# Retention and a snake-activated feed-forward on one core: the place of one transpose among the loads, and of one square beside the last weight load

## The chip, the cores and the metric

The kernel runs on 1 core of one Trainium2 chip. The metric is the device time of one execution in microseconds (us). The core has five engines that this text names: TensorE (PE in the profile; its weight loads are PEld), VectorE (DVE), ScalarE (ACT), GpSimd (POOL) and SyncE (SP), which here does nothing but issue DMAs. Each engine works through its own list of instructions in order, and an instruction waits until what it needs has been done elsewhere.

## The reference: what is computed

Eight batches of a decayed causal attention without softmax (8 heads, 576 positions, 64 wide), then a feed-forward over the 4608 rows that come out:

```python
scores = scale * np.matmul(q, k.transpose(0, 1, 3, 2))
Dmat = np.where(rel >= 0, gamma[:, None, None] ** rel[None, :, :], 0.0)
x = np.matmul(scores * Dmat[None], v)        # then (batch, seq, heads * dim)
h = x @ w_in                                 # 4608 x 512 by 512 x 2048
s = np.sin(alpha * h)
g = h + s * s / (alpha + 1e-09)
out = g @ w_out                              # 2048 x 512
```

## The kernel before, in words

The 576 positions of a batch are taken as two parts of 256 (p = 0 and 1) and a rest of 64. The decay is put into q and k while they are cast to 16 bits (`cast`, L158), so scores need only a triangular mask; what lies over 128 positions back goes through running sums of k times v (`outer`, `more`, `to_state`, `add_states`).

**Attention of a batch b.** `load(b, nm, p)` (L137) issues the DMA of one part of q, k or v into a "raw" buffer, 512 KB; for k and v of batches 4 and later it is four DMAs of 128 KB. `cast` makes the 16-bit copy. q and k are then needed turned: in batches 0 and 1 TensorE does it (`turn`, L221, with `take` copying out), from batch 2 on a transposing DMA from SyncE (`crossed`, L213, issued at L217), which writes the tiles kT and qT. `scores` (L362) reads kT and qT of one part, `masked` multiplies by the mask on VectorE, `values` and `add_states` sum up the output, and `keep` puts it into xT, 512 rows of the feed-forward's input.

**Feed-forward of a block n** (512 rows, the main parts of batch n). For each of 16 feature chunks fc: `project` (L541) multiplies xT by a chunk of w_in, four matmuls; `sine` (L554) on ScalarE; `square` (L562) on the engine that is its third argument (A_ ScalarE, V VectorE, G_ GpSimd); `product` (L571) on VectorE, which writes the chunk of gT and frees the PSUM bank that `project` took. `gemm2(n, u, tag)` (L587) multiplies four chunks of gT by four rows of chunks of w_out: u = 4c + part, where part 3 reads chunks 12 to 15. `finish` copies the result out and stores it.

**The weights.** w_in and w_out come in quarters by DMAs that GpSimd issues and that turn 32 into 16 bits on the way (`load_w_in` L107, `load_w_out` L111). Quarter g of w_out is its chunks 4g to 4g + 3, so `load_w_out(3)` brings what part 3 of each `gemm2` reads; the first of these is `gemm2(0, 15)` (L843), then `gemm2(0, 7)` (L847).

**What sets the order.** Up to the middle of block 2 the order is written out by hand under `tc.manual_schedule()` (from L656): the calls stand in the order in which each engine is to take them, and each engine keeps the order of its own calls. From block 3 on a loop (L1140) places them. SyncE's list holds all loads of q, k and v, all transposing DMAs, the stores of `finish` and a few tiny DMAs named `gate` that hold SyncE back until a weight quarter has come (`wait_for_w_in`, `wait_for_w_out`). GpSimd's list holds casts, running sums, some squares and the weight loads. Which raw buffer a load takes is fixed by a string of digits (`BUFFERS`, L18); a load waits until the cast of the buffer's last content is done.

**Around the change.** In block 0, L790 to L803: chunk 10, its square on GpSimd, `load_w_out(3)`, `wait_for_w_in(3)` on SyncE, then chunk 14 with its square on ScalarE, chunk 12, and the first scores of batch 1. On SyncE, behind `wait_for_w_in(3)` stand the loads of batch 1's v part 0 (L811), k part 1 (L824) and v part 1 (L832); the cast of that k (L825) feeds `turn(1, "k", 1)` (L835) on TensorE. Around L869 to L880 SyncE issues the four transposes of batch 2 (k part 1, q part 1, k part 0, q part 0) with the load of batch 4's q part 1 ahead of the last, then loads of batches 3 and 4. The turned q part 0 of batch 2 is first read by `at[2].scores(0, 0, "m0")` (L947), behind `project(1, 0)` on TensorE; the load of batch 4's q part 1 is first read by `cast(4, "q", 1, G_)` (L997).

Of the kernel before, what the change touches and what calls it, by code (L numbers as in the profile page):

```python
# [35 lines left out]
def kernel(  # L36
# [68 lines left out]
    V, A_, G_ = nc.vector, nc.scalar, nc.gpsimd  # L105
# [5 lines left out]
    def load_w_out(g):  # L111
        nc.gpsimd.dma_start(w_out16[:, 4 * g : 4 * g + 4, :], w_out_r[:, g])

    def halves(n):
        return slice(64 * n, 64 * n + 64)
# [10 lines left out]
    def place(tag, shape, dtype):  # L126

        name = tag + next(slot_of[tag])
        if name not in places:
            places[name] = work.tile(shape, dtype, tag=name, bufs=1, name=name)  # L130
        return places[name]
# [5 lines left out]
    def load(b, nm, p):  # L137
        if p < 2 and b >= HALVED and nm != "q":
            t_ = place("raw", [P, H, 2 * D], F32)
            for g in range(2):  # L140
                for r in range(2):
                    s0 = 256 * p + 128 * g + 64 * r
                    nc.sync.dma_start(
                        t_[halves(g), :, r * D : r * D + D], src[nm][b, :, s0 : s0 + 64, :].rearrange("h i d -> i h d")
                    )
        elif p < 2:
            t_ = place("raw", [P, H, 2 * D], F32)
            nc.sync.dma_start(  # L148
                t_, src[nm][b, :, 256 * p : 256 * p + 256, :].rearrange("h (i r) d -> i h (r d)", r=2)
            )  # L150
        else:
            if b % 2 == 0:
                raw[b, nm, 2] = work.tile([P, H, D], F32, tag="raws", bufs=3, name=nm + "s32")
            t_ = raw[b - b % 2, nm, 2]
            nc.sync.dma_start(t_[halves(b % 2)], src[nm][b, :, 512:576, :].rearrange("h i d -> i h d"))
        raw[b, nm, p] = t_
# [47 lines left out]
    def new_T(b, nm, p):  # L204
        if (b, nm, p) not in T:
            T[b, nm, p] = (
                place(nm + "T", [P, 8, P], F16)
                if p < 2
                else work.tile([P, 4, P], F16, tag=nm + "Ts", bufs=B // 2, name=nm + "Ts")
            )  # L210
        return T[b, nm, p]

    def crossed(b, p, nms="kq"):  # L213
        for nm in nms:
            x = half[b, nm, p]
            x = x.rearrange("p a r t d -> p (a r t d)") if p < 2 else x.rearrange("p a t d -> p (a t d)")
            nc.sync.dma_start_transpose(new_T(b, nm, p), x)  # L217
# [323 lines left out]
    def project(n, fc, tag, part=None):  # L541

        if n not in gT:
            gT[n] = work.tile([P, FC, 512], F16, tag="gT", bufs=2, name="gT")
        if (n, fc) not in hps_of:
            hps_of[n, fc] = [bank(tag), None]
        cols = PART[part]
        for a in range(KT):
            matmul(  # L549
                hps_of[n, fc][0][:, cols], w_in16[fc // 4][:, a, fc % 4 :: 4], xs[n][:, a, cols],  # L550
                start=(a == 0 and part != 1), stop=(a == KT - 1), skip_group_check=True,
            )

    def sine(n, fc):  # L554
        hps = hps_of[n, fc][0]
        s_t = place("s", [P, 512], F16)
        nc.scalar.activation(  # L557
            s_t, hps, mybir.ActivationFunctionType.Sin, bias=0.0, scale=alpha_t[:, fc : fc + 1],
        )
        hps_of[n, fc][1] = s_t  # L560

    def square(n, fc, eng):  # L562
        s_t = hps_of[n, fc][1]
        ss_t = place("ss", [P, 512], F16)
        if eng is nc.scalar:
            nc.scalar.activation(ss_t, s_t, mybir.ActivationFunctionType.Square)  # L566
        else:
            eng.tensor_tensor(ss_t, s_t, s_t, MULT)  # L568
        hps_of[n, fc][1] = ss_t
# [41 lines left out]
    def wait_for_w_in(g):  # L611

        nc.sync.dma_start(gate, w_in16[g][:, 0, 0:64])
# [42 lines left out]
    with tc.manual_schedule():  # L656
# [133 lines left out]
        project(0, 10, "m0")  # L790
        sine(0, 10)
        square(0, 10, G_)
        load_w_out(3)
        wait_for_w_in(3)
        product(0, 5)
        project(0, 14, "h2")
        sine(0, 14)
        square(0, 14, A_)
        project(0, 12, "h1")
        sine(0, 12)  # L800
        at[1].scores(0, 0, "m1")
# [70 lines left out]
        cast(2, "k", 0, V)  # L872
        crossed(2, 1, "q")
        crossed(2, 0, "k")
        load(4, "q", 1)
        crossed(2, 0, "q")
        load(3, "v", 0)
        load(3, "v", 1)
        load(4, "v", 0)
# [381 lines left out]
```

## Time and profile before

| | us |
|---|---|
| median of 3 runs | 307.51 (306.63 to 307.99) |
| the profiled execution: its own time | 309.48 |
| the profiled execution: span of the trace | 307.5 |
| TensorE busy in the span | 293.8 |
| ScalarE, VectorE, GpSimd busy | 193.8, 190.1, 136.4 |

The profile is of one execution. Its page gives busy times by engine, the span in 40 slices with the clock that TensorE was granted (PEclk) and what the DMA engines moved, the chain of work that ended last, and groups of instructions. Other views of the same trace list an engine's instructions in order of time, with the idle time ahead of each and what ended it in brackets, or sum them over stretches. L numbers are lines of the kernel. A DMA's time from issue to landing is told where some instruction waited for it.

### The profile page before, as it was taken

What the parts mean: (1) busy time and instruction counts of PE and PEld (TensorE: products, weight loads), DVE (VectorE), ACT (ScalarE), POOL (GpSimd) and SP (SyncE); (2) the same over time, 40 slices, a digit from 0 to 9 for tenths busy, and PEclk for the clock granted to TensorE, in tenths of its full rate; (3) what the DMA queues carried; (4) which work ended last, traced back from release to release, by engine and by line L of the source; (5) the groups of instructions that cost most, each with busy time, mean ns of one, the idle gap of its engine ahead of it and who ended that gap; (6) DMA issues with size and microseconds to landing.
All of it is one profiled execution on the core that took longest, in us unless ns stands there. A gap on an engine that the chain in (4) does not pass through costs nothing.

```text
span 307.5 us, 7881 instructions
## 1 busy us (share of the span) xinstructions
PE 293.8 (96%) x3208; PEld 156.1 (51%) x3208; DVE 190.1 (62%) x280; ACT 193.8 (63%) x322; POOL 136.4 (44%) x151
## 2 busy tenths in 40 slices
PE   5889979969999999999999999999999999999995
PEld 4566445534554645454545444544455454444443
DVE  2678858766538786657764676566656746655600
ACT  1669916957686887684678567756774456555411
POOL 4793579472498686669058708563030000000000
PEclk9999999989999999999999999999999999999999
DMA  7999999998898688999597879877361121111133
GB/s 223 348 221 212 265 285 308 189 260 237 193 223 143 141 166 179 271 143 189 127 255 164 195 158 269 165 119 179 83 132 38 38 44 39 36 34 34 42 92 74
DMA packets 120484, 50.05 MB, mean 163 GB/s; under 512 B 80384, under 2 KB 115456, under 8 KB 120448
## 3 DMA queue, kind: packets, MB, share of 16 engines
q1 hardware_dynamic: 116928, 45.17, 62.6%
q0 software_dynamic: 2688, 4.19, 7.5%
q8 instruction: 25, 0.41, 0.6%
q10 hardware_dynamic: 832, 0.18, 0.3%
q14 instruction: 11, 0.09, 0.1%
HBM read 36.75 MB, written 9.44 MB: 150 GB/s over the span
## 4 chain that ended last, share of the span: by engine, by line
PE 82%; DMA 10%; POOL 3%; SPq 2%; issue 1%; ACT 0%; DVE 0%; DVEq 0%; ACTq 0%; POOLq 0%
PE ops L592 39%; PE hps L549 36%; DMA w_in<-in_moe_w_in_dram 4%; PE o L414 2%; DMA qT<-q 2%; SPq L148 2%; PE sc L372 2%; DMA raw<-in_q_dram 2%; DMA raw<-in_v_dram 2%; POOL q L194 1%; PE kv L308 1%; PE o L436 1%; POOL k L194 1%; POOL v L121 0%; PE os L497 0%
## 5 line engine op out<-in xcount | busy, mean ns | idle before, releaser
L573 DVE SCALAR_TENSOR_TENSOR gT<-ss,inva,hps 128x512 f16<-128x512 f16 x144 | 106.0, 745 | 64.0 <-ACT ss L566 58.9
L592 PE MATMUL ops<-w_out,gT 128*128 128x512 f16 (+2 forms) x592 | 142.5, 374 | 0.1
L557 ACT ACTIVATE s<-hps,alpha_t 128x512 f16<-128x512 f32 x144 | 97.6, 685 | 70.4 <-PE hps L549 68.3
L549 PE MATMUL hps<-xT,w_in 128*128 128x512 f16 (+1 forms) x532 | 127.5, 375 | 0.7 <-DMA w_in<-in_moe_w_in_dram 0.7
L549 PEld LDWEIGHTS <-w_in 128*128 128x128 f16 x596 | 66.9, 114 | 59.8 <-issue 2.0
L592 PEld LDWEIGHTS <-gT 128*128 128x128 f16 x592 | 56.0, 98 | 62.3 <-issue 0.4
L566 ACT ACTIVATE ss<-s 128x512 f16<-128x512 f16 x73 | 45.9, 631 | 1.4
L568 DVE TENSOR_TENSOR ss<-s 128x512 f16<-128x512 f16 x63 | 33.2, 528 | 20.4 <-ACT s L557 19.8
L194 POOL TENSOR_TENSOR k<-raw,cn 128x1024 f16<-128x1024 f32 (+1 forms) x17 | 30.5, 1795 | 27.1 <-DMA raw<-in_k_dram 27.1
L119 ACT COPY osb<-ops 128x512 f32<-128x512 f32 (+1 forms) x34 | 19.7, 580 | 16.6 <-PE ops L592 15.1
L194 POOL TENSOR_TENSOR q<-raw,cn 128x1024 f16<-128x1024 f32 x13 | 24.5, 1902 | 2.1 <-DMA raw<-in_q_dram 2.0
L384 DVE TENSOR_TENSOR ret<-sc,mask 128x1024 f16<-128x1024 f32 x16 | 19.1, 1218 | 3.7 <-PE sc L372 3.6
L353 POOL TENSOR_TENSOR s<-kvs,cn 128x256 f32<-128x256 f32 x21 | 13.3, 633 | 10.6 <-ACT kvs L119 10.4
L354 POOL TENSOR_TENSOR kvs<-s,kvs 128x256 f32<-128x256 f32 x21 | 15.3, 727 | 4.2 <-ACT kvs L119 1.7
L549 PE MATMUL hps<-xS,w_in 128*128 128x512 f16 x64 | 16.4, 379 | 0.0
L121 POOL CAST v<-raw 128x1024 f16<-128x1024 f32 x10 | 10.3, 1036 | 11.5 <-DMA raw<-in_v_dram 10.6
L384 DVE TENSOR_TENSOR ret<-sc,mask_halved 128x768 f16<-128x768 f32 x16 | 15.2, 949 | 0.0
L178 POOL TENSOR_TENSOR ks<-ks,cn 128x512 f16<-128x512 f32 x4 | 4.2, 1042 | 22.7 <-DMA vs<-in_v_dram 11.4
L119 ACT CAST xT<-o 128x1024 f16<-128x1024 f32 (+1 forms) x15 | 12.9, 878 | 1.7 <-PE o L436 1.6
L372 PE MATMUL sc<-qT,kT 64*64 64x128 f16 (+1 forms) x512 | 10.7, 219 | 2.5 <-DMA qT<-q 2.4
L346 POOL TENSOR_TENSOR s<-kvs,cn 128x256 f16<-128x256 f32 x17 | 10.9, 645 | 4.6 <-ACT kvs L119 3.0
L372 PEld LDWEIGHTS <-kT 64*64 64x64 f16 x512 | 7.8, 111 | 9.7 <-issue 8.4
(58 smaller groups left out, 148.3 us busy)
## 6 DMA issues: line engine op xcount, KB each, us to landing
out_dram<-osb SPq DMA_DIRECT2D x70, 128.0 KB, 2.5
raw<-in_q_dram SPq DMA_DIRECT2D x16, 512.0 KB, 5.9
raw<-in_k_dram SPq DMA_DIRECT2D x8, 512.0 KB, 6.1
raw<-in_v_dram SPq DMA_DIRECT2D x8, 512.0 KB, 6.2
raw<-in_v_dram SPq DMA_DIRECT2D x32, 128.0 KB, 3.2
raw<-in_k_dram SPq DMA_DIRECT2D x32, 128.0 KB, 3.3
w_in<-in_moe_w_in_dram POOLq DMA_DIRECT2D x4, 512.0 KB, 11.7
w_out<-in_moe_w_out_dram POOLq DMA_DIRECT2D x4, 512.0 KB, 13.0
```

The source lines that it names most:

```text
L119: eng.copy(d_, s_)
L194: eng.tensor_tensor(dst[:, a0:a1].rearrange("p a r t d -> p t (a r) d"), t_.rearrange("p (t a) x -> p t a x", t=2)[:, :, a0:a1].rearrange( ...
L353: nc.gpsimd.tensor_tensor(s32, self.kvs[:, c - 1], g1.unsqueeze(2).to_broadcast([P, 4, D]), MULT)
L354: nc.gpsimd.tensor_tensor(self.kvs[:, c], s32, self.kvs[:, c], ADD)
L372: matmul(sc[halves(g), t, c : c + n], kT[halves(t), 2 * a + r, halves(g)], qT[halves(t), 2 * a : 2 * a + 2, 64 * g + i0 : 64 * g + 64], st ...
L384: nc.vector.tensor_tensor(ret.rearrange("p t (z x) -> p (t z) x", z=2)[:, :, 0:n], sc.rearrange("p t (z x) -> p (t z) x", z=2)[:, :, 0:n], ...
L549: matmul(hps_of[n, fc][0][:, cols], w_in16[fc // 4][:, a, fc % 4 :: 4], xs[n][:, a, cols], start=(a == 0 and part != 1), stop=(a == KT - 1 ...
L557: nc.scalar.activation(s_t, hps, mybir.ActivationFunctionType.Sin, bias=0.0, scale=alpha_t[:, fc : fc + 1],)
L566: nc.scalar.activation(ss_t, s_t, mybir.ActivationFunctionType.Square)
L568: eng.tensor_tensor(ss_t, s_t, s_t, MULT)
L573: nc.vector.scalar_tensor_tensor(gT[n][:, fc, :], ss_t, inva[:, fc : fc + 1], hps, MULT, ADD)
L592: matmul(ops[n, c, cols.start][:, cols], gT[n][:, fk, c * P : (c + 1) * P], w_out16[:, fk, cols], start=(fk == 0), stop=(fk == FC - 1), sk ...
```

## The change

Two moves. The square of chunk 14 of block 0 goes from ScalarE to GpSimd, and `load_w_out(3)`, on GpSimd's list, comes behind that square instead of ahead of it; `wait_for_w_in(3)` is on SyncE's list and stands where it stood there. And on SyncE's list the load of batch 4's q part 1 comes behind the transpose of batch 2's q part 0 instead of ahead of it. The raw buffers and the s and ss buffers are taken in the same order as before.

```diff
@@ -790,12 +790,12 @@
         project(0, 10, "m0")
         sine(0, 10)
         square(0, 10, G_)
-        load_w_out(3)
         wait_for_w_in(3)
         product(0, 5)
         project(0, 14, "h2")
         sine(0, 14)
-        square(0, 14, A_)
+        square(0, 14, G_)
+        load_w_out(3)
         project(0, 12, "h1")
         sine(0, 12)
         at[1].scores(0, 0, "m1")
@@ -872,8 +872,8 @@
         cast(2, "k", 0, V)
         crossed(2, 1, "q")
         crossed(2, 0, "k")
+        crossed(2, 0, "q")
         load(4, "q", 1)
-        crossed(2, 0, "q")
         load(3, "v", 0)
         load(3, "v", 1)
         load(4, "v", 0)
```

## The prediction, made before the changed kernel was run

> **What bounds the kernel now.** First the page: the busy times and the span in 40 slices.
>
> ```profile
> PE 293.8 (96%) x3208; PEld 156.1 (51%) x3208; DVE 190.1 (62%) x280; ACT 193.8 (63%) x322; POOL 136.4 (44%) x151
> ...
> PE   5889979969999999999999999999999999999995
> ...
> PEclk9999999989999999999999999999999999999999
> ```
>
> TensorE is the bound: busy 293.8 us or 96% of the span, with the other engines under two thirds. It has holes only in the first quarter, and one slice there has a clock of 8 tenths. A change of a wait pays only where TensorE stands idle, so next I read TensorE in order of time there (start, duration, instruction, idle ahead of it and its releaser).
>
> ```profile
> 42.78 0.62 PE L227 MATMUL tr<-ident,k 128*128 128x128 f16 x8 [1.65 <-POOL k L194]
> ...
> 44.76 1.04 PE L592 MATMUL ops<-w_out,gT 128*128 128x512 f16 x4
> ...
> 66.99 0.64 PE L372 MATMUL sc<-qT,kT 64*64 64x128 f16 x16 [2.37 <-DMA qT<-q]
> ```
>
> Two holes: 1.65 us ahead of the turning of batch 1's k part 1, and 2.37 us ahead of `scores(0, 0)` of batch 2, which waits for the transposed q. The change touches both. The second, from 64.62 (66.99 - 2.37), costs more than its length. The stretches with the granted clock (the number behind POOL's) show it:
>
> ```profile
> 40.00:50.00 10.00, 8.25 (x184) 4.38 (x182) 6.67 (x9) 3.73 (x9) 8.21 (x8) 1.00 1.07 315
> ...
> 67.00:71.00 4.00, 4.00 (x26) 1.77 (x27) 1.88 (x2) 1.44 (x3) 3.69 (x7) 0.58 0.88 216
> ```
>
> Right behind the hole the clock is 0.58 of full over 4 us. Twelve projection matmuls take 4.08 us on the chain of work, where four take 0.86 elsewhere on it:
>
> ```profile
> 31.86 5.84 DMA raw<-in_v_dram
> ...
> 59.79 7.06 DMA qT<-q
> 67.63 4.08 PE hps L549 x12
> ...
> 95.21 0.86 PE hps L549 x4
> ```
>
> 3 x 0.86 = 2.58, so the slow clock costs 1.50 us. Hole and clock together: 2.37 + 1.50 = **3.87 us**. The hole of 1.65 us left the clock at full (the stretch from 40 to 50).
>
> **The second move: the transpose ahead of the load.** SyncE's list around it:
>
> ```profile
> 57.80 1.26 SPq L217 DMA_TRANSPOSE kT<-k  x1
> 59.16 0.54 SPq L148 DMA_DIRECT2D raw<-in_q_dram  x1
> 59.79 1.99 SPq L217 DMA_TRANSPOSE qT<-q  x1
> 61.88 2.26 SPq L148 DMA_DIRECT2D raw<-in_v_dram  x2
> ```
>
> SyncE issues without a gap here, so its pace, and no wait, sets these times. GpSimd has cast that q by 52.2 (50.27 + 1.90):
>
> ```profile
> 50.27 1.90 POOL L194 TENSOR_TENSOR q<-raw,cn 128x1024 f16<-128x1024 f32 x1
> ...
> 82.63 3.76 POOL L194 TENSOR_TENSOR q<-raw,cn 128x1024 f16<-128x1024 f32 x2
> ```
>
> The transpose is issued at 59.16 instead of 59.79: 0.63 us won by issue alone. More lies behind: ahead of it in the same queue are no longer 512 KB. What the queue moved from 58 to 62 us, in slices of 0.1 us:
>
> ```profile
> GB/s 289 257 294 292 289 289 108 161 289 289 289 274 262 282 279 276 292 289 353 266 259 88 39 49 67 77 54 108 123 97 97 102 56 61 143 113 179 230 102 108
> ```
>
> The transposes run at some 290 GB/s up to 60.1, then the load that stands between them begins at under 150. The last transpose has its data behind that load. It lands 7.06 us after its issue, while the page says what others take:
>
> ```profile
> kT<-k SPq DMA_TRANSPOSE x12, 5.0
> qT<-q SPq DMA_TRANSPOSE x12, 3.9
> ```
>
> Bounds for the moved one: 59.16 + 3.9 = 63.1, + 5.0 = 64.2, and + 7.06 = 66.2 if the load was not the reason. I take 3.9, since it now follows a transpose directly. TensorE is there at 64.62, so the hole is gone in the first two cases, and with it the slow clock: -3.87. In the third the hole shrinks by 0.63 to 1.7, which is the length of the hole that left the clock full: between -0.63 and -2.1. The load itself comes some 2 us later; its cast starts at 82.63 (the second row above), so nothing waits for it. The loads behind it keep their issue times, since the same instructions stand ahead of them.
>
> [...]
>
> What TensorE needs next, 3.87 us earlier? VectorE and ScalarE get their work from TensorE here. The first loads it meets are batch 3's v, issued by 64.1 (61.88 + 2.26). The two loads of that size below take 5.84 and 8.3, which makes 70 to 72.4. Their casts on ScalarE stand at 76.46, now 72.6:
>
> ```profile
> 76.46 1.56 ACT L119 CAST v<-raw 128x512 f16<-128x512 f32 x2
> ```
>
> Then come batch 3's transposes:
>
> ```profile
> 78.22 2.71 SPq L143 DMA_DIRECT2D raw<-in_k_dram  x4
> 81.44 0.40 SPq L148 DMA_DIRECT2D raw<-in_q_dram  x1
> ...
> 85.23 0.54 SPq L148 DMA_DIRECT2D raw<-in_q_dram  x1
> 86.42 1.38 SPq L217 DMA_TRANSPOSE qT<-q  x1
> ...
> 93.38 1.34 SPq L217 DMA_TRANSPOSE qT<-q  x1
> ```
>
> ```profile
> 93.60 0.64 PE L372 MATMUL sc<-qT,kT 64*64 64x128 f16 x32
> ...
> 100.32 0.42 PE L372 MATMUL sc<-qT,kT 64*64 64x128 f16 x16
> ```
>
> The scores at 93.60 move to 89.73 and read the q issued at 86.42. That issue waits for a GpSimd cast, which comes earlier with TensorE, but SyncE is itself nearly full from 60 on. What it can win are its gaps ahead of 81.44 (0.51 behind 78.22 + 2.71) and 86.42 (0.65 behind 85.23 + 0.54), of which some 0.1 each is no wait. So it issues at 85.5: + 3.9 gives 89.4, in time by 0.3; with 5.0 it would be late by 0.8. The scores at 100.32 move to 96.45; their q, issued at 93.38 by the same list, now at 92.4, lands at 96.3 to 97.4: late by 0 to 0.95. I take **+0.3** for this; its ends are 0 and, if SyncE gains nothing at all (93.38 + 3.9 to 5.0 against 96.45), 0.8 to 1.9. Later transposes hang on stores, which follow TensorE.
>
> **The first move: square and w_out's last quarter.** GpSimd's list:
>
> ```profile
> 33.39 1.04 POOL L568 TENSOR_TENSOR ss<-s 128x512 f16<-128x512 f16 x1 [0.57 <-ACT s L557]
> 34.37 0.60 POOL L112 DMA_DIRECT2D w_out<-in_moe_w_out_dram  x1
> 37.76 1.03 POOL L121 CAST v<-raw 128x1024 f16<-128x1024 f32 x1 [2.79 <-DMA raw<-in_v_dram]
> 38.76 0.60 POOL L346 TENSOR_TENSOR sS<-kvs,cn 128x256 f16<-128x256 f32 x1
> 40.82 1.90 POOL L194 TENSOR_TENSOR k<-raw,cn 128x1024 f16<-128x1024 f32 x1 [1.45 <-DMA raw<-in_k_dram]
> ```
>
> ```profile
> 33.92 0.63 ACT L566 ACTIVATE ss<-s 128x512 f16<-128x512 f16 x1
> ```
>
> ```profile
> 35.42 1.40 DVE L573 SCALAR_TENSOR_TENSOR gT<-ss,inva,hps 128x512 f16<-128x512 f16 x2
> ```
>
> The moved square takes 1.04 instead of 0.63, from 34.4, when GpSimd comes to it (its sine is done by 33.92, where ScalarE's square began), to 35.4. GpSimd has 2.79 us free ahead of 37.76, which hides it. ScalarE is rid of 0.63. The product waits to 35.45 where it began at 35.42: under 0.1, which VectorE makes up in its next idle time, and without that it would be 0.1 on the path. So these instructions cost nothing.
>
> What counts is that w_out's quarter is issued at 35.4, 1.05 us later. The loads of batch 1 move beside it. The k's time to landing; what was moved from 34 to 42 us, in slices of 0.2 us, with the last quarter's time; and the times of all four quarters of w_out:
>
> ```profile
> raw<-in_k_dram SPq DMA_DIRECT2D x1, 512.0 KB, 8.3
> ```
>
> ```profile
> GB/s 85 210 335 282 346 344 284 318 323 341 348 346 351 346 351 361 420 259 266 233 225 253 225 266 205 187 225 228 128 243 305 310 348 346 305 305 310 330 343 348
> ...
> w_out<-in_moe_w_out_dram POOLq DMA_DIRECT2D x1, 512.0 KB, 7.4
> ```
>
> ```profile
> DMA to landing us min/median/max: 7.4/13.0/15.8
> ```
>
> The v, 5.84 us in the chain above, lands at 37.70; the k 3.1 us behind it at 40.8, though issued (8.3 before) only 0.6 behind. The quarter moved meanwhile: from 37.4 to 39.8 the rate is down at 130 to 270. With it 1.05 later, the k's data may be through before. GpSimd can start on that k at 39.37 (38.76 + 0.60), so the gain at TensorE's first hole is between 0 and 1.45. For the other sign: the quarter is read at 44.76 and landed 7.4 us after its issue, which makes 42.8 now; 44.76 - 1.45 is 43.3, so it is in time. I take **-1.1**, nearer to the full 1.45, since 1.05 us at the 340 GB/s that were moved then is 0.36 MB, over half of that load.
>
> [...]
>
> **Sum.** -3.87 - 1.1 + 0.3 = -4.7. The execution's own time is 309.48 (span 307.5), so 304.8 there; against the median of the runs, 307.51, it is 302.8.
>
> **The rivals.**
> - The k is no earlier, because the quarter shares its engines anyway. For: its 8.3 us. Against: the quarter is 1.05 later. -3.87 + 0.3: 303.9.
> - Batch 3's transposes take the place of the wait: SyncE stays late and the scores at 96.45 wait for 98.3. For: SyncE's list has few gaps. Against: its three waits follow TensorE. -3.87 + 1.9 - (0 to 1.1): 304.4 to 305.5.
> - The swap does not do what it says: the transpose lands 7 us after issue for another reason. -0.63 if the clock still drops, -2.1 if not, and the first move's 0 to -1.1: 304.3 to 306.9.
> - The slow clock stays where it is though the hole is gone, because something other than the hole sets it. For: the hole of 1.65 left it full. Against: it begins with the matmul behind the hole. -2.37 - 1.1 + 0.3: 304.3.
> - Slower: w_out's last quarter comes too late for `gemm2(0, 15)` at 44.76. Place: TensorE's list at L843, with everything behind it. Price: the other quarters took 13.0 in the median and up to 15.8; 35.4 + 13.0 = 48.4 is a hole of 3.6, + 15.8 = 51.2 one of 6.4, each with the slow clock's 1.5 behind it: 3.6 + 1.5 - 3.87 + 0.3 = +1.5 and +4.3, 309.0 to 311.8. It decides from a landing near 48.4; one in 44.8 to 47 eats a part of the gain. Against: this quarter took 7.4, and it starts when no other quarter is left.
>
> **How the numbers follow.** Chances: forecast 0.41 (302.0 to 303.6), k no earlier 0.23, batch 3's transposes 0.13, slow clock stays 0.03, no effect of the swap 0.12, slower 0.08. Predicted 302.8. The range goes from 301.8 (-3.87 - 1.45 with no new wait is 302.2, and the runs spread by some 0.5 around their median) to 306.4, which leaves out a part of the third rival and the slower one. Faster by over 0.5% (1.5 us, about what a measurement can tell from no change) takes the first four cases and a third of the fifth: 0.84; same 0.08; slower 0.08.
>
> **What would show it.** Right: no idle time ahead of `scores(0, 0)` near 63 to 65 us, no slice of PEclk at 8; the transposed q lands under 5 us after its issue; GpSimd starts the k cast near 39.5 and the first hole is under 0.6 us. Wrong: a new idle time ahead of scores near 89 or 96, or ahead of L592 near 43.

## The result

The changed kernel takes 305.9 us in the median of 21 runs (303.88 to 311.41), against 307.59 for the kernel before, run beside it (21 runs, 305.43 to 309.5). That is 1.7 us less. The ratio is 0.9953, 95% interval 0.993 to 0.9976; it leaves out 1, but is just under the 0.5% that the forecast took as what a measurement can tell from no change. Executions over 1.5% above the fastest of their kernel are left out of all ratios, here two of the changed kernel's 21 (309.04 and 311.41); with them the means are 306.46 and 307.53, a ratio of 0.9965. Forecast were 4.7 us and 302.8.

The profiled execution after has an own time of 305.86 and a span of 303.9; before, 309.48 and 307.5. So this one pair shows -3.6 us, twice what the medians show. Most of what follows is about that difference.

The page of after, the lines that answer to those of before (busy times, TensorE's share in the 40 slices, its granted clock):

```profile
span 303.9 us, 7880 instructions
...
PE 292.6 (96%) x3208; PEld 156.2 (51%) x3208; DVE 189.2 (62%) x280; ACT 193.9 (64%) x321; POOL 136.5 (45%) x152
...
PE   6789989999999999999999999999999999999995
...
PEclk9999999999999999999999999999999999999999
```

ScalarE has one instruction less and GpSimd one more. The slice with a clock of 8 tenths is gone. TensorE in order of time (start, duration, instruction, idle ahead of it and its releaser):

```profile
41.52 0.62 PE L227 MATMUL tr<-ident,k 128*128 128x128 f16 x8
...
43.84 1.02 PE L592 MATMUL ops<-w_out,gT 128*128 128x512 f16 x4 [0.27 <-DMA w_out<-in_moe_w_out_dram]
...
46.22 0.45 PE L308 MATMUL kv<-v,k 64*64 64x64 f16 x32 [1.35 <-ACT v L119]
...
65.04 0.42 PE L372 MATMUL sc<-qT,kT 64*64 64x128 f16 x16
65.39 2.78 PE L549 MATMUL hps<-xT,w_in 128*128 128x512 f16 x12
```

Both holes of before are gone: there is no idle time ahead of the turning at 41.52 or of the scores at 65.04, and the twelve projection matmuls behind those scores take 2.78 where they took 4.08. Two new waits stand between: 0.27 us for w_out's last quarter and 1.35 us for the cast of a v. Together they are 1.62 us, as much as the first hole was (1.65). The chain of work of after names the v's load behind that cast:

```profile
33.50 11.60 DMA raw<-in_v_dram
45.12 1.05 ACT v L119
...
65.46 2.71 PE hps L549 x12
```

What the two moves did by themselves can be read on their engines. SyncE's list of after, then the DMA view of its window from 58 to 60 us (the number is the time from issue to landing):

```profile
57.61 1.26 SPq L217 DMA_TRANSPOSE kT<-k  x1
58.97 1.25 SPq L217 DMA_TRANSPOSE qT<-q  x1
60.27 0.58 SPq L148 DMA_DIRECT2D raw<-in_q_dram  x1
```

```profile
qT<-q SPq DMA_TRANSPOSE x1, 3.3
```

The transpose was issued at 58.97 and landed at 62.3, almost 3 us ahead of the scores; before it was 59.79 and 7.06. GpSimd's list of after, then the DMA view of its window from 31 to 38 us:

```profile
33.80 2.04 POOL L568 TENSOR_TENSOR ss<-s 128x512 f16<-128x512 f16 x2 [0.57 <-ACT s L557]
35.78 0.60 POOL L112 DMA_DIRECT2D w_out<-in_moe_w_out_dram  x1
...
39.57 1.89 POOL L194 TENSOR_TENSOR k<-raw,cn 128x1024 f16<-128x1024 f32 x1
```

```profile
raw<-in_k_dram SPq DMA_DIRECT2D x2, 512.0 KB, 6.7
w_out<-in_moe_w_out_dram POOLq DMA_DIRECT2D x1, 512.0 KB, 8.0
```

The quarter is issued at 35.78 instead of 34.37, the k lands 6.7 us after its issue instead of 8.3, and its cast begins at 39.57 without a wait. Each move did what it was meant to do in this trace.

### The profile page after: what moved, and what is told of

It reads as the page before. It is cut to its first block, busy times and chain, and to the rows that moved or that the text cites. A ratio compares the mean times of both kernels' runs of the same rounds, so it can differ in the third digit from the quotient of the medians.

```text
span 303.9 us, 7880 instructions
## 1 busy us (share of the span) xinstructions
PE 292.6 (96%) x3208; PEld 156.2 (51%) x3208; DVE 189.2 (62%) x280; ACT 193.9 (64%) x321; POOL 136.5 (45%) x152
## 3 DMA queue, kind: packets, MB, share of 16 engines
q0 software_dynamic: 2688, 4.19, 7.7%
## 4 chain that ended last, share of the span: by engine, by line
PE 85%; DMA 10%; ACT 1%; POOL 1%; SPq 1%; issue 1%; DVE 0%; DVEq 0%; ACTq 0%
PE ops L592 39%; PE hps L549 39%; DMA raw<-in_v_dram 4%; DMA w_in<-in_moe_w_in_dram 4%; PE o L414 2%; DMA raw<-in_k_dram 2%; PE sc L372 2%; PE kv L308 1%; SPq L148 1%; PE o L436 1%; POOL k L194 1%; ACT s L557 0%; ACT v L119 0%; POOL w_in L109 0%; PE os L497 0%
## 5 line engine op out<-in xcount | busy, mean ns | idle before, releaser
L194 POOL TENSOR_TENSOR k<-raw,cn 128x1024 f16<-128x1024 f32 (+1 forms) x17 | 28.8, 1696 | 26.2 <-DMA raw<-in_k_dram 25.6
L568 POOL TENSOR_TENSOR ss<-s 128x512 f16<-128x512 f16 x9 | 9.2, 1039 | 6.2 <-ACT s L557 6.2
L119 ACT CAST v<-raw 128x1024 f16<-128x1024 f32 (+1 forms) x6 | 5.8, 976 | 9.8 <-DMA raw<-in_v_dram 9.8
```

Of the source, the lines that this page charges most:

```text
L119: eng.copy(d_, s_)
L194: eng.tensor_tensor(dst[:, a0:a1].rearrange("p a r t d -> p t (a r) d"), t_.rearrange("p (t a) x -> p t a x", t=2)[:, :, a0:a1].rearrange( ...
```

## The experiments

**The theories.** A: the terms of the forecast were those of one execution that stood far above the median; typical executions stall less, so there is less to win. B: the moves win what was forecast, and batch 3's transposes, late by more than the forecast's 0.3, give most of it back. C: one of the two moves has no effect, or harms.

### Each move alone, and both kernels again

The edits are the two hunks of the diff, one at a time: r2 has only the second (transpose ahead of the load), r3 only the first (square and w_out's quarter); r1 is the kernel before, r4 the whole change.

> The kernel before, unchanged, looked at again with the granted clock of each execution. Theory A (the prediction's sum was made on an execution that is not typical: the slow clock behind the hole ahead of scores comes in some executions alone): the trace has the hole of 2 to 3 us near 65 us again, but most executions show a granted clock over 0.995 and the profiled time is 1 to 2 us under 309.5. Theory B (the slow clock is always there and the gain went elsewhere): a clock of about 0.994 in nearly every execution, twelve projection matmuls of 4.08 us behind the hole. Time the same as before in both, ratio 1.000 within 0.003.

> The second move alone: the transpose of batch 2's q part 0 ahead of the load of batch 4's q part 1; square and w_out's last quarter as before. Theory A: no idle time ahead of scores near 65 us, and 1.5 to 2.5 us faster than before, which is the hole without the slow clock; as fast as the whole change. Theory B: the slow clock goes too, -3.5 to -4 us in the runs. The prediction on record has -3.87 + 0.3 for this part. Theory C (the first move costs what the second wins): this one is 1 us or more faster than the whole change.

> The first move alone: the square of chunk 14 on GpSimd and w_out's last quarter issued behind it; SyncE's list as before. The prediction on record: -1.1 us. Theory A: the first hole only moves, from ahead of the turning of k (1.65 us) to ahead of the outer product (1.35) and of the product with w_out (0.27), because v part 1 lands 2 us later: 0 +- 0.4 us. Theory C: 1 us or more slower than before, the hole near 65 us being longer.

> The whole change again, on the same chip as its two parts. Theory A: the sum of the two parts, -1.5 to -2.5 us against before, with a trace that again has no idle time ahead of scores near 65 us and 1.3 to 1.9 us of it near 43 to 46. Theory B: -3.5 us. Theory C: 1 us or more slower than the second move alone.

| | median us | ratio to before | 95% interval |
|---|---|---|---|
| r1, before | 308.76 | 1.0034 | 1.0 to 1.0067 |
| r2, second move alone | 306.66 | 0.9967 | 0.993 to 1.0005 |
| r3, first move alone | 307.93 | 0.9993 | 0.9957 to 1.0029 |
| r4, both | 306.13 | 0.9965 | 0.993 to 1.0 |

Before's median beside these four is 307.38. r2 is 0.7 us under it and r4 1.2, where theory A had 1.5 to 2.5 for both and B 3.5 or more. The rows also show how far two runs of one kernel can lie apart: r1 is the kernel before, unchanged, and its median is 1.4 us above. So a difference of 0.3% in one run says little; that the whole change is faster rests on four runs of it that agree (0.9953, 0.9965, and 0.9968 and 0.9949 below).

r1's trace says more. TensorE, then the chain of work:

```profile
65.17 0.42 PE L372 MATMUL sc<-qT,kT 64*64 64x128 f16 x16 [1.85 <-DMA qT<-q]
...
90.90 0.64 PE L372 MATMUL sc<-qT,kT 64*64 64x128 f16 x32 [0.60 <-DVE ss L568]
```

```profile
58.12 6.91 DMA qT<-q
65.59 2.71 PE hps L549 x12
```

No hole near 42 us, a second hole of 1.85, and the twelve matmuls behind it at full clock (2.71). This execution took 306.86 us, 2.6 less than the one that the forecast was built on. In r3 the transpose is as late as before, and the stretch behind it (the granted clock stands behind the busy time of POOL) shows this:

```profile
66.11 0.42 PE L372 MATMUL sc<-qT,kT 64*64 64x128 f16 x16 [2.68 <-DMA qT<-q]
...
92.66 0.64 PE L372 MATMUL sc<-qT,kT 64*64 64x128 f16 x32 [1.45 <-DMA qT<-q]
```

```profile
67.00:71.00 4.00, 4.00 (x49) 2.03 (x48) 2.28 (x4) 3.35 (x6) 3.11 (x6) 1.00 0.76 158
```

A hole of 2.68, longer than the 2.37 of the forecast, and the clock stays full. For the second move, theory C is out by the traces: the second hole is there without it and gone with it. In r4, with both moves, only one wait is left, on batch 3's scores:

```profile
89.69 0.64 PE L372 MATMUL sc<-qT,kT 64*64 64x128 f16 x32 [1.35 <-DMA qT<-q]
```

### Before once more, the second move alone, and the whole change

> The second move alone, again, beside the whole change on one chip. In six traces the k load of batch 1 landed 6.7 us after issue in all that have the first move, and 6.7 or 8.3 to 9.4 in those that have not. Theory E (the first move takes away the k's late landing, which comes in a part of the executions only, and pays with v's): this one shows a first hole of 1.6 to 2.8 us in a part of its executions, and its mean time is 0.3 to 1.2 us over the whole change's, with more spread. If the first move is worth nothing: equal means within 0.3.

> The whole change once more, as the measure for the other three on this chip: 1.2 to 2 us under before, no idle time near 65 us, 0 to 1.4 us near 43 to 46 us and 0 to 1.4 us near 90 us.

> The kernel before, one look: which of its waits is in a typical execution. The prediction took 1.65 us ahead of batch 1's turning, 2.37 us ahead of batch 2's scores and 1.50 us of slow clock behind from one trace. Theory A: the wait of batch 2's scores is there again (1.5 to 2.8 us), the slow clock behind it and the first hole are not both. If the one trace was typical: both are there again.

> The kernel before, a further look, with the same question: the wait of batch 2's scores 1.5 to 2.8 us; the first hole either under 0.3 us, with batch 1's k landing 6.7 us after issue, or over 1.5 us, with 8.3 us or more.

> The whole change, as the measure for it on the same chip: 1 to 1.7 us under before.

The second move alone gave 0.9992 (0.9946 to 1.0038) this time, the whole change 0.9968 (0.9932 to 1.0004) in r12 and 0.9949 (0.9916 to 0.9982) in r16. The mean of r11 lies 1.0 us over that of r12 (307.48 against 306.48), as theory E expected. Its trace, of an execution of 305.36 us, has a first hole of 0.37 only, no second one, and this:

```profile
89.54 0.64 PE L372 MATMUL sc<-qT,kT 64*64 64x128 f16 x32 [1.14 <-DMA qT<-q]
```

r13 and r14 are one execution of before each, 309.34 and 310.3 us. The second hole of 1.5 to 2.8 us that was expected is smaller in both. r13, TensorE, then the stretches from 40 to 48 us, and its k's time to landing:

```profile
43.71 0.62 PE L227 MATMUL tr<-ident,k 128*128 128x128 f16 x8 [2.59 <-POOL k L194]
...
68.08 0.42 PE L372 MATMUL sc<-qT,kT 64*64 64x128 f16 x16 [0.90 <-DMA qT<-q]
```

```profile
40.00:44.00 4.00, 1.41 (x12) 0.59 (x9) 1.21 (x3) 0.72 (x1) 2.25 (x2) 1.00 1.10 322
44.00:48.00 4.00, 4.00 (x46) 1.78 (x43) 2.17 (x4) 0.33 (x1) 2.70 (x5) 0.57 1.04 307
```

```profile
raw<-in_k_dram SPq DMA_DIRECT2D x2, 512.0 KB, 9.2
```

Here the k is late by more, the slow clock stands behind the **first** hole, and the second hole is down to 0.90 because TensorE itself comes later. r14 has a third pattern:

```profile
42.14 0.62 PE L227 MATMUL tr<-ident,k 128*128 128x128 f16 x8 [1.02 <-POOL k L194]
...
65.20 0.42 PE L372 MATMUL sc<-qT,kT 64*64 64x128 f16 x16 [1.22 <-DMA qT<-q]
...
93.00 0.71 PE L372 MATMUL sc<-qT,kT 64*64 64x128 f16 x32 [2.66 <-DMA qT<-q]
```

In r16, the whole change, four small waits come together and the execution takes 306.92:

```profile
41.24 0.62 PE L227 MATMUL tr<-ident,k 128*128 128x128 f16 x8 [0.17 <-POOL k L194]
...
45.50 0.45 PE L308 MATMUL kv<-v,k 64*64 64x64 f16 x32 [1.24 <-ACT v L119]
...
64.69 0.42 PE L372 MATMUL sc<-qT,kT 64*64 64x128 f16 x16 [0.21 <-DMA qT<-q]
...
91.22 0.64 PE L372 MATMUL sc<-qT,kT 64*64 64x128 f16 x32 [1.39 <-DMA qT<-q]
```

These rows make a ledger. For each profiled execution it has TensorE's idle times in three places, an estimate of 1.50 us (the prediction's price) for each slow stretch of the clock behind a hole, and what its own time is without them.

| | own time | 40 to 48 us | 62 to 70 | 88 to 104 | slow clock | left |
|---|---|---|---|---|---|---|
| before, the forecast's | 309.48 | 1.65 | 2.37 | 0 | 1.50 | 303.96 |
| before, r1 | 306.86 | 0 | 1.85 | 0.60 | 0 | 304.41 |
| before, r13 | 309.34 | 2.59 | 0.90 | 0 | 1.50 | 304.35 |
| before, r14 | 310.30 | 1.02 | 1.22 | 2.66 | 1.50 | 303.90 |
| first move alone, r3 | 308.13 | 0.17 | 2.68 | 1.45 | 0 | 303.83 |
| second move alone, r11 | 305.36 | 0.37 | 0 | 1.14 | 0 | 303.85 |
| both, after | 305.86 | 1.62 | 0 | 0 | 0 | 304.24 |
| both, r4 | 305.26 | 0 | 0 | 1.35 | 0 | 303.91 |
| both, r12 | 305.46 | 0 | 0 | 1.24 | 0 | 304.22 |
| both, r16 | 306.92 | 1.41 | 0.21 | 1.39 | 0 | 303.91 |

The last column is the same within 0.6 us, while the own times differ by 5. So these executions differ by their stalls in these three places and by little else, and 304.1, the mean of that column, is about the time without them. The traces of r5 to r10 and r15 fit as well, from 303.72 (r15) to 304.41 (r10); r2's needs a fourth place, which is told further down. Against the medians, a typical execution of before stalls for about 307.59 - 304.1 = 3.5 us, one of after for 305.9 - 304.1 = 1.8. The forecast's execution stalled for 5.52.

### Batch 3's transposes ahead of a gate and a load

If theory B holds, taking away the wait near 90 us should bring back the missing microseconds. r5 adds this to the change (r6 does it without the first move):

```diff
-        wait_for_w_in(3)
-        load(4, "q", 0)
         crossed(3, 1, "q")
         crossed(3, 0, "k")
+        wait_for_w_in(3)
+        load(4, "q", 0)
         load(4, "k", 1)
```

> The whole change, and the same move once more for batch 3: on SyncE's list the transposes of its q part 1 and k part 0 come ahead of the tiny gate and of the load of batch 4's q part 0. Theory A (what the hole near 65 us gives is taken back by the wait of batch 3's scores near 90 us, since SyncE cannot follow): that wait, 1.35 us in the trace of the whole change on this chip, is gone or under 0.3, and the time is 0.7 to 1.5 us under the whole change's, 2 to 3 us under before. Theory B (the gain went elsewhere, to the slow clock alone): the time stays within 0.4 us of the whole change's 306.1.

> The second move and its repetition for batch 3, without the first move (square on ScalarE, w_out's last quarter issued ahead of it). If the first move is worth nothing, as the look at it alone says (ratio 0.999), this is as fast as the kernel with all three, within 0.4 us. The prediction on record has the first move at -1.1 us: then this is about 1 us slower than that one.

Both came out slower than before: r5 310.73 us, 1.0141 (1.01 to 1.0182); r6 310.28, 1.0102 (1.0054 to 1.015). The wait near 90 was gone. r5's GpSimd and TensorE show what stands in its place:

```profile
93.92 1.90 POOL L194 TENSOR_TENSOR q<-raw,cn 128x1024 f16<-128x1024 f32 x1 [4.19 <-DMA raw<-in_q_dram]
...
98.42 1.90 POOL L194 TENSOR_TENSOR k<-raw,cn 128x1024 f16<-128x1024 f32 x1
```

```profile
97.56 0.42 PE L372 MATMUL sc<-qT,kT 64*64 64x128 f16 x16 [0.92 <-DMA qT<-q]
...
100.37 0.44 PE L308 MATMUL kv<-v,k 64*64 64x64 f16 x32 [2.15 <-POOL k L194]
```

The load that now comes behind the transposes feeds `cast(4, "q", 0, G_)`; GpSimd waits 4.19 us for it, and the cast of a k that stands behind it in GpSimd's list makes TensorE wait 2.15, with a slow clock behind (0.50 from 101.5 to 104.7 us). With r5's 1.37 ahead of kv at 46.00 its ledger is 310.34 - 1.53 - 3.07 - 1.50 = 304.24 (1.53 with a 0.16 at 41.54). In r6, which lacks the first move, a first hole of 2.78 with its own slow clock (0.57 from 44 to 48 us) comes on top.

r10 (and r15, the same kernel) takes the cause away: to r5 it moves that one cast on GpSimd's list to behind `square(2, 13, G_)`. r9 keeps the load ahead and moves only the gate behind the transposes:

```diff
-        cast(4, "q", 0, G_)
...
         square(2, 13, G_)
+        cast(4, "q", 0, G_)
```

```diff
-        wait_for_w_in(3)
         load(4, "q", 0)
         crossed(3, 1, "q")
         crossed(3, 0, "k")
+        wait_for_w_in(3)
```

> The whole change with the tiny gate DMA (w_in's last quarter, long landed) behind batch 3's transposes of q part 1 and k part 0 instead of ahead of the load before them: SyncE comes 0.65 to 1.0 us earlier to that load and to the transposes, in the same order. Theory A (SyncE's list, not TensorE, sets when batch 3's q is there): the wait of the scores near 90 us is 0.6 to 1.0 us shorter than in the whole change, and the time 0.4 to 1.0 us under the whole change's. If that wait were set by something else, no change within 0.4 us.

> The kernel with batch 3's transposes ahead of the load of batch 4's q part 0, which came out 4 us slower than the whole change since GpSimd stood 4.2 us at the cast of that load with the cast of batch 4's k behind it. Here that cast comes behind the cast of k and a square on GpSimd. Theory A (GpSimd's order was the new wait): the 2.15 us ahead of the outer product near 100 us are gone, no slow clock there, and the time is 0.5 to 1.5 us under the whole change's. If the transposes' place itself was harmful: still 3 us or more over the whole change.

> The whole change with batch 3's transposes ahead of the load of batch 4's q part 0 and that load's cast behind the cast of batch 4's k: again, to tell it from the whole change, which it beat by 0.8 us in the mean with intervals that overlap. Theory A (part of the gain was taken back by batch 3's wait): 0.4 to 1.2 us under the whole change again. If that was chance: within 0.3 us of it.

r10 gave 306.29 us, 0.9933 (0.9891 to 0.9976), and its repeat r15 307.52, 0.9994 (0.9961 to 1.0027), which is 4.4 and 3.2 us under r5's median. So the cast was most of what r5 lost. But r16 beside r15 has 0.9949, so this kernel isn't shown to beat the change; its two runs lie 0.6% apart. r9 gave 306.49, 0.9986 (0.9947 to 1.0025), beside r12's 306.48. TensorE of r9 and of r10:

```profile
88.91 0.64 PE L372 MATMUL sc<-qT,kT 64*64 64x128 f16 x32 [0.51 <-DVE ss L568]
```

```profile
96.29 0.42 PE L372 MATMUL sc<-qT,kT 64*64 64x128 f16 x16 [0.97 <-DMA qT<-q]
```

The wait near 90 can be taken away, and then the next one shows: 0.51 for a square on VectorE, or 0.97 for the next q on SyncE's list. No time was gained that these intervals (some 0.8% wide) can show. Theory B, as the main cause, is out: there are not 3 us behind that wait. What the wait does cost, within the intervals, stays open.

### The second move the other way

r7 is the kernel before with a second load ahead of the transpose:

```diff
         load(4, "q", 1)
-        crossed(2, 0, "q")
         load(3, "v", 0)
+        crossed(2, 0, "q")
```

> The kernel before with two loads instead of one ahead of the transpose of batch 2's q part 0 (the load of batch 3's v part 0 too). Theory A (each load of 512 KB ahead of it in the queue is what makes it late): the hole near 65 us grows by 1 to 2 us, to 3 to 4.5 us, the transpose lands 1 us or more later, and the slow clock behind the hole comes in most executions since the hole is longer; 2 to 4 us slower than before, less what batch 3's scores no longer wait. Theory D (the transpose is late for another reason than the load): the hole grows by 0.6 us at most, what SyncE needs to issue the load.

It gave 309.95 us, 1.0065 (1.0009 to 1.012). TensorE, and the chain of work:

```profile
43.72 0.62 PE L227 MATMUL tr<-ident,k 128*128 128x128 f16 x8 [2.70 <-POOL k L194]
...
69.06 0.42 PE L372 MATMUL sc<-qT,kT 64*64 64x128 f16 x16 [1.39 <-DMA qT<-q]
```

```profile
61.41 7.51 DMA qT<-q
```

The transpose lands 7.51 us after its issue, against 6.35 to 7.06 in the five traces with one load ahead, so the second load adds little to the first; the 1 us or more of theory A isn't shown. The hole is only 1.39 because this execution had a first hole of 2.70 with a slow clock behind it (0.83 from 40 to 50 us), which made TensorE late as well. That first hole is not of r7's edit, so its ratio can't be put down to the load alone.

### The slower rival, made to happen

r8 is the change with w_out's last quarter issued later still:

```diff
         square(0, 14, G_)
-        load_w_out(3)
...
         cast(1, "v", 0, G_)
+        load_w_out(3)
```

> The whole change with w_out's last quarter issued later still, behind the cast of batch 1's v part 0 on GpSimd, near 39 us instead of 35.5. With the 6.3 to 8.0 us that this quarter took to land in the traces so far, it lands near 45.3 to 47 and the product that reads it first waits 1.5 to 3 us; batch 1's v part 1 lands 2 us earlier than in the whole change and nothing waits for it. 1 to 2.5 us slower than the whole change. If the quarter's place decides nothing (the rival that DMA engines share whatever is there), the time is within 0.5 us of the whole change.

It gave 309.2 us, 1.0071 (1.0031 to 1.0112): slower than before, and over 1% (some 3 us) slower than the whole change in its four runs, where 1 to 2.5 us were expected. TensorE:

```profile
46.80 1.86 PE L592 MATMUL ops<-w_out,gT 128*128 128x512 f16 x4 [2.54 <-DMA w_out<-in_moe_w_out_dram]
```

Four matmuls take 1.86 behind the hole, where they take 1.02 in after: the slow clock stands here too. The trace also has 0.77 us ahead of the turning of k and 0.83 ahead of batch 3's scores. The place of the slower rival (a hole at L843, and the slow clock behind it) was right. Its bound was not: the quarter landed at 46.8 (issued at 39.06, 7.70 to landing), where the forecast had a landing at 44.8 to 47 eat only a part of the gain. The change itself stops short of it, with a wait of 0.27.

## Why the prediction was wrong

The direction was right, and in the pair of traces each move did what it was meant to do in the place that was forecast. The size was wrong by 3.1 us (305.9 against 302.8), and that splits in two.

- **The step that failed: "so 304.8 there; against the median of the runs, 307.51, it is 302.8."** The execution stood 1.97 us above the median, and the forecast took the same 4.7 off both. But what put it above the median were the stalls that the change removes: it had 5.52 us of them, a typical execution 3.5. The excess was taken off twice. The ledger would have stopped it: 302.8 lies below the 304.1 that is left when none of these stalls remains, and below the lowest of the 57 executions of the changed kernel (303.88). This makes 2.0 of the 3.1.
- **-3.87 for the second move.** It was paid in full in the pair of traces: hole and slow clock are both gone. As a typical value it was too large; this is a good part of the same 2.0, read by its term. In four executions of before the hole was 2.37, 1.85, 0.90 and 1.22, 1.6 in the mean, and the slow clock stood behind it in one of the four. By that the move is worth 1.6 + 1.5 / 4 = 2.0. Even this may be too much: the four executions take 309.0 us in the mean, above the median as well, and the second move by itself was 0.7 us (r2) and 0.2 (r11) under before in the medians; r11's interval ends at 1.7. The 1.14 us that r11's trace waits for batch 3's q may be a part of the difference; the rest stays open. The bounds on the moved transpose held: 3.3 us from issue to landing, ahead of the 3.9 that was taken.
- **-1.1 for the first move.** The k did come earlier (6.7 from 8.3, and 6.3 or 6.7 in every trace with this move; 6.7 to 9.4 without it), against the rival that it shares its engines with the quarter in any order. In after nothing was gained, since 0.27 for the quarter and 1.35 for the next v took its place; the forecast had looked at the k and the quarter, not at the v issued behind them. It is the main part of the other 1.1 of the 3.1 (305.86 against 304.8); the +0.3 below, which didn't come in that trace, and 0.28 by which the ledger's last column differs between the pair cancel. That the v is late because the quarter now shares the engines with it is argued, not shown. It was waited for in three of the ten traces with this move (after, r5 and r16), and in these three the quarter took 7.9 to 8.0 us to land, in six of the other seven 6.3 to 6.9.
- **+0.3 for batch 3's transposes.** Near 90 us the four executions of before waited 0, 0.60, 0 and 2.66, the four of after 0, 1.35, 1.24 and 1.39: 0.8 and 1.0 in the mean. The wait is there, but it was often there before (r1's 0.60 is for a square on VectorE, not for a transpose), so in the mean it grew by 0.2. That this is near the forecast's 0.3 says little: it is four traces each, and after, the one set beside the forecast's, has no wait there. The rival's 1.9 on top did not come.
- **The rivals.** "The swap does nothing" and "the slow clock stays" are out: the transpose lands in 3 to 5 us with the swap (4.86 in r16's chain of work at the most), in 6.4 to 7.1 with the load ahead of it, and no slow stretch followed there. The slower one is real but lies further off (r8).

**Where the gain of 1.7 us comes from.** The lists of times say more than the medians. Of 133 executions of before that were run beside these kernels, 51 took over 308 us and 29 under 306.5; with the whole change 5 of 57 and 32; with the second move alone 10 of 24 and 11; with the first alone 6 of 12 and 3. So the second move by itself makes more executions fast, and only both together take away most of those over 308. A list of 12 from one run is weak evidence: r1's 12, of the kernel before and not among the 133, have 8 over 308 and none under 306.5. The ratios of the moves alone (0.9967, 0.9992 and 0.9993) are each too near to 1, with intervals too wide, to say how the gain divides.

The mean granted clock of an execution tells something of the slow stretches. One stretch of 3.4 us at half clock, the length that the last section measures, lowers it by 1.7 / 307.5, to 0.994, as in before, r13, r5, r7 and r8; three would lower it to 0.983, r14's value. Of the 24 executions of the second move alone, 11 have 0.992 to 0.994 or 0.981 to 0.983, among them 9 of the 10 over 308 us. Of before it is 39 of the 112 for which the clock is known (30 of the 45 over 308), of the whole change 9 of 57. So the second move alone made such stretches no rarer, and both moves together did; the 1.50 us that the forecast counted for the second move doesn't show in its runs.

Where these stretches stand the mean clock can't tell. r13 and r7 suggest that they stand behind the hole of a late k, which the first move prevents. That is argued, and it isn't the only way over 308. The one trace of such an execution with the second move alone, r2's of 309.77 us, has its k after 6.7 us and no hole near 42. There one instruction on VectorE took 3.58 us, where it takes 0.42 or 0.43 in the other 17 traces, and TensorE waited for it, with a slow stretch behind (the next 56 matmuls of `project` take 10.50 us, in r1 8.95):

```profile
20.13 3.58 DVE L346 TENSOR_TENSOR s<-kvs,cn 128x256 f16<-128x256 f32 x1
```

```profile
23.77 0.31 PE L436 MATMUL o<-qT,s 64*64 64x128 f16 x8 [3.15 <-DVE s L346]
```

With 1.30 us in two waits for batch 3's q (93.93 and 100.94), its ledger is 309.77 - 3.15 - 1.30 - 1.50 = 303.82, like the others. Neither move touches this stall, and why the instruction took so long is open.

## What to carry to other kernels

Before a gain is summed from one profiled execution, set its own time beside the median: if it stands above, part of what the change would remove is that execution's own, and must not be subtracted from the median as well. A ledger (own time less the bottleneck engine's idle times and slow stretches) over a few executions gives the time that removing such stalls can reach, here 304.1 to within some 0.4 us. In r5, two transposes moved ahead of a load made the load late: GpSimd waited 4.19 us for it and TensorE 2.15 behind that, and the kernel came out slower than before (1.0141). So look at the whole list behind a moved instruction.

## What the runs showed of the hardware

The slow clock isn't decided by the length of a hole alone. It followed holes of 2.15 (r5), 2.37 (the forecast's execution), 2.46 and 2.78 (both r6), 2.54 (r8), 2.59 (r13), 2.66 (r14), 2.70 (r7) and 3.15 us (r2), but not those of 2.68 (r3) or 1.85 (r1). Behind r14's hole four matmuls take 1.89 us, where four take 1.03 some 3 us later; behind r6's 2.46 eight take 2.98, where eight take 1.92 at 108.33; for the others the clock or such a time stands above. Why r5's 2.15 us was enough and r3's 2.68 was not is not shown. In the forecast's execution the slow stretch begins with the matmul behind the hole, at 66.99:

```profile
66.90:67.00 0.10, 0.01 (x4) 0.04 (x4) 0.00 (x0) 0.00 (x0) 0.10 (x1) 0.86 1.12 338
67.00:70.30 3.30, 3.30 (x23) 1.45 (x24) 1.88 (x2) 0.77 (x2) 3.04 (x5) 0.50 0.90 228
70.30:70.40 0.10, 0.10 (x2) 0.00 (x0) 0.00 (x0) 0.10 (x1) 0.05 (x1) 0.57 1.01 230
```

That is 3.4 us at half clock. Three more traces give the same length: 0.57 over 4 us in r13 and in r6 is 0.43 x 4 / 0.5 = 3.4, and 0.83 over 10 us in r7 is 0.17 x 10 / 0.5 = 3.4. In r5 the stretch doesn't begin with the matmul behind the hole, but 1.1 us behind the hole's end at 100.37:

```profile
97.80:101.40 3.60, 1.45 (x96) 1.08 (x86) 1.53 (x2) 0.47 (x1) 3.51 (x4) 1.00 0.88 204
101.50:104.70 3.20, 3.20 (x31) 1.26 (x33) 2.07 (x3) 1.58 (x6) 2.10 (x4) 0.50 1.28 122
```

In r16 a slow clock near the start cost nothing that the ledger shows: its page has this line, with 5 tenths in the second slice, and its ledger ends at 303.91 like the others.

```profile
PEclk9599999999999999999999999999999999999999
```

The same load took different times from one execution to the next: batch 1's k landed 6.7 us after its issue in r1 and 9.2 in r13, with the same kernel.
